# A drain of GpSimd's pipe behind each of its additions, in a planned attention-and-mixer kernel

## The chip, the cores and the metric

One core of a Trainium2 chip runs the kernel. It has five engines, each with an instruction queue of its own: TensorE (PE; its weight loads are listed as PEld), VectorE (DVE), ScalarE (ACT), GpSimd (POOL) and SyncE (SP), which issues most DMAs. The metric is the device time of one execution in microseconds (us); lower is better. Three runs of the kernel before gave a median of 793.61 us (793.22 to 793.68).

## The reference

A routed attention is followed by an MLP mixer. Batch 4, 8 heads, sequence 768, head dimension 64, 16 clusters; then model width 512, token width 256, channel width 1536. All in float32.

```python
q_assign = np.argmax(np.einsum('bhsd,hcd->bhsc', q_n, c_n), axis=-1)
k_assign = np.argmax(np.einsum('bhsd,hcd->bhsc', k_n, c_n), axis=-1)
mask = q_assign[:, :, :, None] == k_assign[:, :, None, :]
scores = scale * np.matmul(q, k.transpose(0, 1, 3, 2))
scores = np.where(mask, scores, -1000000000.0)
...
attn = attn / (np.sum(attn, axis=-1, keepdims=True) + 1e-09)
out = np.matmul(attn, v)
...
xt = x.transpose(0, 2, 1)
h = np.maximum(xt @ w_tok1, 0.0) @ w_tok2
u = x + h.transpose(0, 2, 1)
h2 = np.maximum(u @ w_ch1, 0.0) @ w_ch2
return u + h2
```

`x` is the attention's output with the heads side by side, 4 x 768 x 512.

## The kernel before

The kernel works out a whole program first and then plays it out. Each operation is added to a `Program` with the engines that may take it, a cost for each, and the buffers that it reads and writes. `plan()` then goes through them as a list scheduler does: TensorE's operations keep the order in which they were added; for the other engines it takes, at each moment, the ready operation with the earliest due time, and gives it to an engine that would finish it first. `Program.run` issues the result, so every engine's order is fixed before anything runs. Costs are a constant and a part per element, from the table `COST`; `cost(e, n)` reads it. The scheduler holds GpSimd's and VectorE's operations on arena operands apart, since it counts the two as sharing a port.

All data stand in one buffer of the on-chip memory, the arena, and in eight PSUM banks (`ps`). Stages in order of time: attention in 16 pairs of heads (to some 350 us), token mixing (`token1`, `token2`, to some 405 us), then for each of two groups of two batches `channel1` and `channel2`, the two channel matrices. Every one of these four products is done by a Strassen-like scheme of seven `product` calls. Each `product` is itself such a scheme of seven smaller ones: its four sums T1 to T4 of the right-hand operand are made by `tsum`, its weights come from DRAM through a ring of eight buffers, and for each of its seven parts three matmuls of 128x384 go into PSUM, which VectorE (or ScalarE) then evacuates, mostly by adding what is there already. The sums use two sets of buffers in turn.

GpSimd takes part only here. In `channel1` it makes all `tsum` sums and the `combine` sums between the products (T3, T4, `a` plus `c`, `c` plus `b`, and some of T1 and T2); in `channel2` it makes the `tsum` sums of the first two products, and VectorE the others. Each of its additions covers 128x384 float32, in the arena, and all go through the helper `tt` at L881, whose instruction is at L883: 179 of them. Behind its last sums of a group, `channel2` has VectorE overwrite the matrices that those sums read (`combine(Hm[0, 0], ...)`, on VectorE), and VectorE's queue holds the evacuations of PSUM that TensorE waits for.

ScalarE does the relus between the two matrices (L890) and, in the same time, a check that the weights are in range (L1888); both are placed by the scheduler too.

Of the kernel before, what the change touches and what calls it, by code (L numbers as in the profile page):

```python
# [55 lines left out]
    "ACT16": (-0.275, 0.001426),  # L56
    "JOIN16": (-0.165, 0.001426),
    "DVE": (0.075, 0.00104),
    "POOL": (0.12, 0.0023),
}  # L60
ISSUE = 0.63
BUS = 240e3
# [660 lines left out]
def kernel(  # L723
# [26 lines left out]
    nc = tc.nc  # L750
# [105 lines left out]
    def cost(kind, n):  # L856
        a, b = COST[kind]
        return a + b * n
# [22 lines left out]
    def tt(dst, a, b, op, n, rd, wr, engines=("DVE",)):  # L881
        def fn(e):
            (nc.vector if e == "DVE" else nc.gpsimd).tensor_tensor(out=dst, in0=a, in1=b, op=op)  # L883

        return g.add({e: cost(e, n) for e in engines}, fn, rd, wr)

# [184 lines left out]
    def route(m, bk):  # L1071
# [13 lines left out]
        def blocks(t):  # L1085
# [3 lines left out]
        vec(lambda: nc.vector.reduce_max(out=mxs.ap[:, 0:24], in_=blocks(a), axis=AX.X), 0.54,  # L1089
            a.k(), mxs.k())  # L1090
        tt(blocks(e), blocks(a), mxs.ap[:, 0:24].unsqueeze(2).to_broadcast([P, 24, C]),
           ALU.is_ge, HS, a.k() + mxs.k(), e.k())
        vec(lambda: nc.vector.transpose(out=o.ap, in_=e.ap), 0.56, e.k(), o.k())
# [107 lines left out]
    def add_up(m):  # L1201
        st = unit[m]
        for n in range(2):
            a = es[n]
            x, y, z = st[HJ * n : HJ * n + HJ]
            tt(a.ap, x.ap, y.ap, ALU.add, 2 * S, x.k() + y.k(), a.k())
            tt(a.ap, a.ap, z.ap, ALU.add, 2 * S, a.k() + z.k(), a.k())
        a, b = es[1], es[0]
        if FOLD[m] == "V":
            tt(a.ap, a.ap, b.ap, ALU.add, 2 * S, a.k() + b.k(), a.k())  # L1210
        if FOLD[m] != "T":
            return

        def fn(e):
            nc.gpsimd.dma_start(
                a.ap.rearrange("p h t -> p (h t)"), b.ap.rearrange("p h t -> p (h t)"),
                accum_op=ALU.add,
            )

        g.add({"POOL": 1.0}, fn, a.k() + b.k(), a.k(), (2.2 * 768 * 1024, 6144))  # L1220
# [812 lines left out]
```

## Time and profile before

| what | value |
|---|---|
| median of three runs | 793.61 us |
| the profiled execution's own time | 794.77 us |
| its span, first to last instruction | 793.0 us |
| TensorE clock granted, mean | 0.999 |
| TensorE's idle time from 370 to 400 and from 400 to 450 us | 0.51 and 0.39 us |
| GpSimd's first and last addition begin at | 374.03 and 699.48 us |
| last instruction of TensorE ends at | 787.4 us |

In the profile, L883 is a line of the kernel; "out<-in" are the names of buffers. An idle time belongs to the instruction behind it and is put down to what ended it ("<-"). The chain of waits goes back from the last instruction, at each step to what released it.

### The profile page before, as it was taken

The page shows a single profiled execution, that of the slowest core. Times are in us where ns is not written, and L with a number is a line of the kernel's source. Part 1 is how long each engine was busy: PE and PEld are TensorE (multiplying, and loading weights), DVE is VectorE, ACT ScalarE, POOL GpSimd, SP SyncE. Part 2 cuts the span into 40 slices and gives each one's busy share as a digit, 9 for nine tenths or more (in the row PEclk, how much of TensorE's full clock was granted, in tenths as well). Part 3 has the DMA queues.
Part 4 walks back from the last instruction along what each step waited for, and adds up shares of the span by engine and source line. Part 5 has one row for each costly group of instructions (what it writes and reads, how often), then busy time and mean ns, then how long its engine had stood idle before and what let it go on. Part 6 is the DMA issues. An engine that isn't in the chain of part 4 may idle for free.

```text
span 793.0 us, 15364 instructions
## 1 busy us (share of the span) xinstructions
PE 780.1 (98%) x5983; PEld 465.4 (59%) x5983; DVE 677.5 (85%) x876; ACT 461.2 (58%) x612; POOL 190.2 (24%) x185
## 2 busy tenths in 40 slices
PE   7999999999999999999999999999999999999997
PEld 6666666666666666544555555555555555555554
DVE  6869999999999999999999967899953567799964
ACT  4688898888898875599714367642245204400422
POOL 0000000000000000001264599700186379830000
PEclk9999999999999999999999999999999999999999
DMA  9576769777678953659858999975788844444767
GB/s 214 154 174 164 183 151 232 205 219 203 162 207 183 273 180 113 182 110 224 184 139 246 312 290 258 270 191 123 167 188 179 170 106 102 100 101 106 162 144 178
DMA packets 326576, 143.68 MB, mean 181 GB/s; under 512 B 260192, under 2 KB 322400, under 8 KB 326496
## 3 DMA queue, kind: packets, MB, share of 16 engines
q1 hardware_dynamic: 324128, 141.83, 71.4%
q8 instruction: 49, 0.80, 0.4%
q10 hardware_dynamic: 2368, 0.79, 0.4%
q14 instruction: 31, 0.25, 0.1%
HBM read 91.95 MB, written 28.61 MB: 152 GB/s over the span
## 4 chain that ended last, share of the span: by engine, by line
PE 88%; DVE 5%; ACT 3%; issue 2%; DMA 1%; SPq 0%; POOL 0%; DVEq 0%; POOLq 0%; ACTq 0%
PE ps L844 72%; PE ps L1226 16%; DVE arena L883 4%; ACT arena L873 2%; DMA wd<-arena 1%; ACT arena L1193 1%; DVE arena L865 0%; DVE arena L1360 0%; SPq L903 0%; DVE arena L1363 0%; ACT arena L863 0%; DVE arena L1366 0%; DVE arena L1356 0%; DVE arena L1280 0%; DVE arena L1273 0%
## 5 line engine op out<-in xcount | busy, mean ns | idle before, releaser
L844 PE MATMUL ps<-arena 128*128 128x384 f32 (+5 forms) x2735 | 642.4, 463 | 7.3 <-DVE arena L865 2.7
L844 PEld LDWEIGHTS ps<-arena 128*128 128x128 f32 (+1 forms) x2351 | 342.3, 185 | 252.8 <-issue 59.5
L883 DVE TENSOR_TENSOR arena<-arena 128x1536 f32<-128x1536 f32 (+6 forms) x350 | 370.2, 1079 | 10.5 <-PE ps L1226 2.3
L883 POOL TENSOR_TENSOR arena<-arena 128x384 f32<-128x384 f32 x179 | 189.5, 1094 | 510.8 <-DVE arena L883 379.4
L883 DVE TENSOR_TENSOR arena<-ps,arena 128x384 f32<-128x384 f32 (+3 forms) x227 | 189.6, 845 | 79.4 <-PE ps L844 75.4
L873 ACT COPY arena<-arena 128x768 uint16<-128x768 uint16 x221 | 189.4, 953 | 61.4 <-DMA arena<-arena 31.9
L1193 ACT ACTIVATE arena<-ps 128x768 f32<-128x768 f32 x192 | 150.6, 811 | 31.6 <-PE ps L844 29.9
L1226 PE MATMUL ps<-arena 128*32 128x192 f32 (+1 forms) x3248 | 144.7, 335 | 0.0
L1226 PEld LDWEIGHTS ps<-arena 128*32 128x32 f32 x3248 | 103.8, 110 | 44.0 <-issue 13.9
L863 ACT COPY arena<-ps 128x384 f32<-128x384 f32 (+2 forms) x41 | 29.5, 728 | 120.6 <-PE ps L844 120.4
L890 ACT ACTIVATE arena<-arena 128x1152 f32<-128x1152 f32 (+1 forms) x38 | 39.9, 1075 | 54.9 <-DVE arena L883 54.5
L1888 ACT ACTIVATE arena<-arena 128x768 f32<-128x768 f32 x40 | 38.7, 970 | 32.7 <-DMA arena<-in_moe_w_ch_dram 24.7
L844 PEld LDWEIGHTS <-arena 64*128 64x128 bf16 x384 | 19.3, 94 | 25.0 <-issue 0.6
L1360 DVE SCALAR_TENSOR_TENSOR arena<-arena 128x512 uint32<-128x512 uint32 (+1 forms) x31 | 20.6, 681 | 0.3
L1097 ACT ACTIVATE arena<-arena 128x384 bf16<-128x384 f32 x16 | 11.2, 703 | 16.1 <-issue 16.1
L1366 DVE SCALAR_TENSOR_TENSOR arena<-arena 128x512 f32<-128x512 uint32 (+1 forms) x31 | 20.2, 671 | 0.4
L1356 DVE TENSOR_SCALAR arena<-arena 128x512 uint32<-128x512 uint32 (+1 forms) x31 | 13.2, 435 | 5.8 <-DMA arena<-in_moe_w_tok_dram 5.8
L1273 DVE STREAM_TRANSPOSE arena<-ps 128x768 f32<-128x768 f32 x16 | 15.3, 955 | 0.0
L1363 DVE TENSOR_SCALAR arena<-arena 128x512 uint32<-128x512 uint32 (+1 forms) x31 | 14.4, 483 | 0.3
L865 DVE COPY arena<-ps 128x384 f32<-128x384 f32 (+3 forms) x12 | 8.0, 666 | 4.7 <-PE ps L844 4.6
L1088 DVE STREAM_TRANSPOSE arena<-ps 128x384 f32<-128x384 f32 x16 | 9.2, 575 | 3.1 <-PE ps L844 3.0
L1280 DVE STREAM_TRANSPOSE arena<-ps 128x384 f32<-128x384 f32 x16 | 9.3, 579 | 1.5 <-PE ps L1226 1.2
(58 smaller groups left out, 53.1 us busy)
## 6 DMA issues: line engine op xcount, KB each, us to landing
arena<-wd SPq DMA_DIRECT2D x196, 192.0 KB, 3.0
wd<-arena SPq DMA_DIRECT2D x84, 224.0 KB, 3.2
arena<-in_moe_w_ch_dram SPq DMA_DIRECT2D x96, 128.0 KB, 3.0
arena<-in_moe_w_ch_dram SPq DMA_DIRECT2D x16, 768.0 KB, 6.0
arena<-in_v_dram SPq DMA_DIRECT2D x16, 384.0 KB, 4.7
out_dram<-arena SPq DMA_DIRECT2D x14, 384.0 KB, 3.6
arena<-in_k_dram SPq DMA_DIRECT2D x13, 384.0 KB, 4.0
arena<-in_q_dram SPq DMA_DIRECT2D x13, 384.0 KB, 4.2
```

The costliest lines, as they stand in the source:

```text
L844: nc.tensor.matmul(dst, lhsT=lhsT, rhs=rhs, start=start, stop=stop, tile_position=pos, is_transpose=tr, skip_group_check=True,)
L863: nc.scalar.copy(out=dst, in_=src)
L873: nc.scalar.copy(out=dst, in_=src)
L883: (nc.vector if e == "DVE" else nc.gpsimd).tensor_tensor(out=dst, in0=a, in1=b, op=op)
L890: nc.scalar.activation(out=dst, in_=src, func=ACT.Relu)
L1193: lambda e, ex=ex, s=s, u=u: nc.scalar.activation(out=ex.ap[:, :, u * HS : (u + 1) * HS], in_=ps[:, 2 * s : 2 * s + 2, 0:HS], func=ACT.Exp ...
L1226: nc.tensor.matmul(dst, lhsT=lhsT, rhs=rhs, start=start, stop=stop, tile_position=pos, skip_group_check=True,)
L1273: lambda: nc.vector.transpose(out=x.ap[:, :, cols].rearrange("p j (c d) -> p c j d", d=32), in_=ps[:, 6:8, 0:HS],),
L1360: vec(lambda: nc.vector.scalar_tensor_tensor(out=TT, in0=hi, scalar=0xC0000000, in1=hh, op0=ALU.bitwise_and, op1=ALU.bitwise_or), 0.14 + 0 ...
L1363: vec(lambda: nc.vector.tensor_scalar(out=hh, in0=TT, scalar1=0xFF800000, scalar2=None, op0=ALU.bitwise_and), f, T.k(), h.k())
L1366: vec(lambda: nc.vector.scalar_tensor_tensor(out=ll, in0=lo, scalar=float(2.0**-52), in1=hh.bitcast(F32), op0=ALU.mult, op1=ALU.mult,), 0. ...
L1888: lambda e, i=i, func=func, bias=bias, n=n, hi=hi: nc.scalar.activation(out=hi, in_=hi, func=func, bias=bias, accum_out=wsum.ap[:, i, n : ...
```

## The change

GpSimd's branch of `tt` issues a drain behind its addition, and the planner's constant for a GpSimd operation goes from 0.12 to 0.2. A drain is an instruction that holds GpSimd's queue until the engine has finished what was issued before it. The drains carry no semaphore, waits or updates; the instructions that depend on an addition still wait for the addition itself.

```diff
@@ COST @@
-    "POOL": (0.12, 0.0023),
+    "POOL": (0.2, 0.0023),
@@ tt @@
         def fn(e):
             (nc.vector if e == "DVE" else nc.gpsimd).tensor_tensor(out=dst, in0=a, in1=b, op=op)
+            if e == "POOL":
+                nc.gpsimd.drain()
 
         return g.add({e: cost(e, n) for e in engines}, fn, rd, wr)
```

Since the planner reads the new constant, the built program differs in more than the drains. TensorE's order is the same. GpSimd has 179 additions in both, 107 of them ahead of its one other late instruction, a load of a flag, before and 105 after. VectorE's order differs from the last part of token mixing on, ScalarE's from the first range checks on, and SyncE's loads of weights and of the range check are interleaved anew.

## The prediction

> **What bounds the kernel now.** I read the page's totals first, then the chain of waits, then stretches of time, then GpSimd's timeline.
>
> ```profile
> span 793.0 us, 15364 instructions
> PE 780.1 (98%) x5983; PEld 465.4 (59%) x5983; DVE 677.5 (85%) x876; ACT 461.2 (58%) x612; POOL 190.2 (24%) x185
> L883 POOL TENSOR_TENSOR arena<-arena 128x384 f32<-128x384 f32 x179 | 189.5, 1094 | 510.8 <-DVE arena L883 379.4
> ...
> 415.33 370.91 PE ps L844 x1154
> 786.24 0.02 issue
> ```
>
> TensorE sets the time. From 415.33 on the chain is one unbroken piece of 1154 matmul records, up to 786.24. GpSimd (POOL) is busy 24% of the span and all its 179 large instructions come from L883, the line the change edits. So the question is whether slower additions on GpSimd can open a hole in those 370.91 us. The next table asks where GpSimd is full.
>
> ```profile
> 370.00:400.00 30.00, 29.49 (x90) 16.38 (x89) 28.87 (x59) 20.91 (x25) 9.00 (x9) 1.00 0.83 193
> 400.00:450.00 50.00, 49.61 (x153) 28.45 (x152) 47.87 (x61) 18.53 (x27) 24.76 (x24) 1.00 0.76 220
> ...
> 449.97:480.13 30.16, 30.16 (x95) 17.81 (x94) 21.38 (x17) 17.24 (x27) 30.15 (x31) 1.00 1.06 281
> 480.13:512.00 31.87, 31.87 (x100) 18.73 (x99) 24.77 (x22) 23.16 (x36) 28.08 (x25) 1.00 0.96 268
> 512.00:571.00 59.00, 59.00 (x185) 34.75 (x184) 57.82 (x66) 19.35 (x33) 0.00 (x0) 1.00 0.71 173
> 571.00:606.00 35.00, 35.00 (x111) 20.44 (x110) 16.34 (x24) 16.93 (x19) 29.06 (x27) 1.00 0.78 178
> 606.00:639.95 33.95, 33.95 (x107) 19.92 (x106) 19.98 (x15) 10.39 (x11) 9.65 (x11) 1.00 0.75 159
> 639.95:702.00 62.05, 62.05 (x194) 36.57 (x193) 46.21 (x37) 18.07 (x16) 58.78 (x56) 1.00 0.45 103
> 702.00:760.00 58.00, 58.00 (x182) 34.03 (x181) 55.63 (x57) 10.40 (x15) 0.00 (x0) 1.00 0.56 129
> ```
>
> Columns after the stretch and its length: busy time of PE, PEld, DVE, ACT, POOL. Two stretches are full on GpSimd: 449.97 to 512 (31+25 = 56 additions, 58.23 us busy of 62.03) and 639.95 to 702 (56 additions, 58.78 of 62.05). They are the second half of the first channel product of each group and the start of the second one. Right behind each, VectorE (DVE) is full: 57.82 of 59.00, and 55.63 of 58.00. TensorE has no idle time in either, so there is nothing to win there, only to lose. In 370 to 450 TensorE idles 0.51 + 0.39 = 0.90 us: all that a luckier order could win before the tail.
>
> **The change, part by part.** *What stays.* TensorE's order is the same instruction for instruction, GpSimd still gets 179 additions, no semaphore is added, and each drain waits for nothing but the pipe. Up to about 400 us every engine's order is the same, so nothing earlier can move.
>
> *The drains.* 179 drains, one behind each addition. What an addition costs now, and what it costs where it can't overlap its predecessor:
>
> ```profile
> 375.99 1.01 POOL L883 TENSOR_TENSOR arena<-arena 128x384 f32<-128x384 f32 x1
> ...
> 377.08 1.00 POOL L883 TENSOR_TENSOR arena<-arena 128x384 f32<-128x384 f32 x1
> ...
> 639.95 38.33 POOL L883 TENSOR_TENSOR arena<-arena 128x384 f32<-128x384 f32 x40 [2.27 <-DVE arena L883]
> 679.19 1.00 POOL L883 TENSOR_TENSOR arena<-arena 128x384 f32<-128x384 f32 x1 [0.91 <-PE ps L844]
> 681.13 8.77 POOL L883 TENSOR_TENSOR arena<-arena 128x384 f32<-128x384 f32 x9 [0.93 <-PE ps L844]
> 690.87 10.73 POOL L883 TENSOR_TENSOR arena<-arena 128x384 f32<-128x384 f32 x6 [0.97 <-PE ps L844]
> ```
>
> 40 in a row take 38.33 us: 0.96 us from start to start, although one takes 1.00 us, so neighbours overlap by 0.04 us. The addition at 377.08 needs the result of the one at 375.99 (the fourth sum T4 reads the second, T2), which ends at 377.00: it starts 0.08 us later, a pitch of 1.09. A drain is at least such a wait. Its own cost shows only at the program's ends:
>
> ```profile
> 0.34 0.10 POOL L2017 MEMSET const-uint8-127<- 128x1 uint8 x1
> ...
> L2017 POOLq DRAIN  x1: 186/186/186, 0.3 to 0.3; - x1
> ...
> L2028 POOLq DRAIN  x3: 34/45/82, 701.7 to 792.7; - x3
> ...
> L883 POOLq EVENT_SEMAPHORE  x11: 17/17/43, 451.9 to 500.8; - x11
> ```
>
> The drain that found work in the pipe ran from 0.30 to 0.49, 0.05 us past the last memset's end (0.34 + 0.10). So behind an addition: 1.00, plus 0.05 until the drain ends, plus the 0.08 of a released start: 1.13. GpSimd also handles 11 separate semaphore waits among the 56 additions of a full stretch; now they run under the addition before, behind a drain they stand bare, each with its 17 ns and another start of 0.08: 11 x 0.10 / 56 = 0.02. I take a pitch of 1.15. Bounds: below 1.03 (1.00 and the shortest drain, 34 ns, the rest overlapped); above 1.21 (1.00, the whole 186 ns as added, and the 0.02). 1.15 sits between, next to the dependent pair's 1.09 and the one drain that had to wait.
>
> The Trainium skill (page "VectorE: DVE Perf Modes", section "The DRAIN you can't avoid") says of the drains at a program's ends that they take a constant 12 ns or so on all five engines. By that figure a drain would add an estimated 0.01 us to the pair's 1.09, and nothing would be lost below; GpSimd's own rows, 34 to 186 ns, are dearer than that here.
>
> *The planner's number.* The kernel orders its own work; it charged an addition 0.12 + 384 x 0.0023 = 1.003 us and now charges 1.083. So it puts VectorE's and ScalarE's dependents 0.08 us per addition later, and other work before them: from about 400 us on, VectorE's sums, evacuations and weight rounding, ScalarE's relus and range checks and SyncE's (SP's) loads are interleaved anew. The moved weight loads have eight ring buffers and the DMA engines' share was 0.45 to 1.06; I cost the moved loads at nothing while the ring covers them. The reordering itself I cost at 0, with bounds of plus and minus the 0.90 us above. What it does cover is GpSimd's lateness up to a pitch of 1.083; beyond, 1.15 - 1.083 = 0.067 us per addition builds up unplanned, 56 x 0.067 = 3.75 us by the end of each full stretch.
>
> *Who is late next.* Behind an addition GpSimd holds the next sums for TensorE; those are handed over some products ahead through two sets of buffers. The tight hand-over is at the end of each full stretch, where VectorE overwrites the matrix that GpSimd's last sums read:
>
> ```profile
> 687.94 1.00 POOL L883 TENSOR_TENSOR arena<-arena 128x384 f32<-128x384 f32 x1
> ...
> 690.10 1.35 DVE L883 TENSOR_TENSOR arena<-arena 128x1152 f32<-128x1152 f32 x1
> ...
> DVE arena L883 <- POOL arena L883: 2.4, 4, 0.6
> L844 PE MATMUL ps<-arena 128*128 128x384 f32 x1146 | 370.5, 486 | 0.4 <-DVE arena L883 0.4
> 694.63 0.56 DVE L883 TENSOR_TENSOR arena<-ps,arena 128x384 f32<-128x384 f32 x1
> ```
>
> VectorE's combination at 690.10 needs the read that ends at 688.94: 1.16 us of slack. VectorE works in order, so queued behind it are the evacuations of the PSUM banks, and TensorE waits for those. One group of six records takes 6 x 370.5 / 1146 = 1.94 us and its evacuation 0.56, so an evacuation may be late by at most 1.38, less two hand-overs; I take 1.2. Lateness that reaches TensorE: 3.75 - 1.16 - 1.2 = 1.4 us per full stretch; VectorE's idle time behind (1.18 and 2.37 us) comes after the hole is made. Other GpSimd work (24.76 of 50.00, 29.06 of 35.00, 9.65 of 33.95) waits for TensorE anyway and costs nothing.
>
> *Sum.* 2 x 1.4 = 2.8 us. The profiled execution took 794.77 us, 1.8 more than its span, and 1.2 more than the median of the runs; on it the sum is 797.6. On the median, 793.61 + 2.8 = **796.4 us**.
>
> **The rivals.** (1) *Not slower:* the new plan covers it. The hole opens only when 56 x (pitch - 1.083) exceeds 1.16 + 1.2, that is from a pitch of 1.125 on. If the drain overlaps a little with the next instruction's wait, the pair's 1.09 is the answer and the time is 793.6. For it: the pair, the new charge, the short drains of 34 to 82 ns. Against: the drain that had to wait outlasted the memset by 0.05 by itself. (2) *Faster:* the new order closes the 0.90 us of holes before 450: 792.7, and so still inside the 0.2% (1.6 us), about what a measurement of this kernel can tell from no change. Against more than that: TensorE is full behind it. Only the tail of 793.0 - 786.24 = 6.8 us is left, with its last stores in a slightly different order. (3) *Dearer, through the operands' port:* of the six additions from 690.87, four took about twice the time (10.73 for six) while VectorE combined arena operands. If GpSimd's lateness pushes four more of its additions under VectorE's combinations in each full stretch, each costs 1.1 more, 4.4 per stretch, with the slack already spent: 2.8 + 8.8, 805 us. For it: GpSimd will run 56 x (1.15 - 0.96) = 10.6 us more per stretch against some 3.5 us of idle time. Against: the plan moves those combinations later as well.
>
> The Trainium skill (page "SBUF — State Buffer", section "SBUF: two separate sides") states that GpSimd and a VectorE instruction with two SBUF inputs lock a shared pair of ports for a whole instruction. The 10.73 us agree with it.
>
> **How the numbers follow.** Main case 0.52; not slower, 0.28; faster or a won order 0.06, of it 0.04 beyond 0.2%; dearer 0.14. The range: below, 793.61 - 0.9 = 792.7; above, a pitch of 1.21 gives 56 x 0.127 = 7.1, less 2.36 is 4.75 per stretch, 9.5 in all: 803.1. The main case's own range is 795.2 to 800. Slower by over 0.2%: nearly all of the main and dearer cases, 0.65; within: 0.31; faster: 0.04.
>
> **What would show it.** Right: additions in a row 1.13 to 1.17 us apart; new TensorE idle time of 1 to 2 us near 500 to 530 and near 690 to 730, released by VectorE evacuations that stand behind a combination waiting for GpSimd; the rest of the chain unbroken. Wrong: a pitch under 1.12 with no hole (rival 1), or over 1.25; additions of 2.1 us much more often than now (rival 3); holes at other places, at 400 to 450 above all, or a wait for a weight load, which would mean that the reordering, not the drain, decides.

## The result, and the profile after

The changed kernel took 800.84 us (median of four runs, 800.45 to 801.42); the kernel before, beside it, 793.64 us. The ratio is 1.0092 with a 95% interval of 1.0074 to 1.0109: slower by 7.2 us, where 2.8 had been forecast. The profiled execution took 801.42 us, 1.8 more than its span; it is the longest of the four.

The page of the changed kernel: its span, busy times, GpSimd's group, and the chain of waits by engine. The last row is the drains' own, from the view of their line (count, shortest/median/longest in ns).

```profile
span 799.6 us, 15534 instructions
PE 782.4 (98%) x5983; PEld 464.6 (58%) x5983; DVE 682.6 (85%) x878; ACT 458.8 (57%) x610; POOL 199.7 (25%) x185
PE 68%; POOLq 15%; DVE 10%; issue 4%; ACT 1%; DMA 1%; ACTq 0%; SPq 0%; DVEq 0%
L883 POOL TENSOR_TENSOR arena<-arena 128x384 f32<-128x384 f32 x179 | 199.0, 1112 | 514.9 <-DVE arena L883 385.1
L885 POOLq DRAIN  x179: 1069/1096/2304, 372.5 to 713.2; - x179
```

The chain that was one piece of TensorE from 415 us on now runs through GpSimd's queue (POOLq, the drains) for 15% of the span and through VectorE for 10%. A drain's row of 1.1 us isn't its price: the row lasts about as long as the addition (1.00 us) that the drain waits for. The price stands between the additions, as the pitch, the time from one start to the next. GpSimd's timeline:

```profile
686.25 1.00 POOL L883 TENSOR_TENSOR arena<-arena 128x384 f32<-128x384 f32 x1 [0.16 <-POOL arena L883]
687.41 1.00 POOL L883 TENSOR_TENSOR arena<-arena 128x384 f32<-128x384 f32 x1 [0.16 <-issue]
...
694.36 1.01 POOL L883 TENSOR_TENSOR arena<-arena 128x384 f32<-128x384 f32 x1 [0.16 <-issue]
695.59 1.00 POOL L883 TENSOR_TENSOR arena<-arena 128x384 f32<-128x384 f32 x1 [0.22 <-POOL arena L883]
```

From 686.25 to 687.41 are 1.16 us from start to start, where it was 0.96 before. The 0.04 us of overlap has become 0.16 us of nothing, and 0.22 where a separate semaphore wait stands in front.

The same full and idle stretches as before, by windows (PE, PEld, DVE, ACT, POOL; granted clock, DMA share, GB/s):

```profile
449.97:512.00 62.03, 62.03 (x194) 36.50 (x193) 43.45 (x35) 41.20 (x65) 53.27 (x51) 1.00 0.98 268
512.00:523.00 11.00, 8.95 (x24) 4.87 (x23) 8.07 (x8) 5.84 (x13) 8.64 (x6) 0.85 0.98 290
523.00:571.00 48.00, 48.00 (x150) 28.28 (x149) 46.75 (x54) 11.90 (x18) 0.00 (x0) 1.00 0.62 140
...
644.00:715.00 71.00, 71.00 (x221) 41.79 (x220) 50.62 (x42) 19.28 (x19) 61.60 (x56) 1.00 0.45 103
715.00:760.00 45.00, 43.10 (x133) 24.87 (x132) 44.61 (x45) 9.50 (x13) 0.17 (x1) 1.00 0.54 123
```

Each of GpSimd's full stretches is longer than its 62 us of before: of the first one's 56 additions, 51 begin by 512, and the second one's take 71.00 us. TensorE is unbroken within the second, and loses time right behind each: 2.05 us of 11.00 at a granted clock of 0.85, and 1.90 of 45.00. TensorE's own timeline has the places:

```profile
499.70 17.90 PE L844 MATMUL ps<-arena 128*128 128x384 f32 x55
519.65 40.68 PE L844 MATMUL ps<-arena 128*128 128x384 f32 x120 [2.05 <-POOL arena L883]
...
719.45 9.94 PE L844 MATMUL ps<-arena 128*128 128x384 f32 x30 [1.37 <-DVE arena L883]
729.92 3.49 PE L844 MATMUL ps<-arena 128*128 128x384 f32 x10 [0.52 <-DVE arena L883]
```

A record takes 486 ns and the next one starts after 323 (370.5 / 1146), so a hole (a stretch in which TensorE stands idle) costs its idle time and 0.16 us: 2.2 at 519.65, 1.5 and 0.7 at 719.45 and 729.92. The 120 records from 519.65 on should take 119 x 0.323 + 0.486 = 38.9 us and take 40.68. The missing 1.7 us are in the first 3.35 of them, at half the clock:

```profile
519.65:523.00 3.35, 3.35 (x6) 1.83 (x7) 3.35 (x4) 2.08 (x4) 1.78 (x1) 0.50 0.87 258
```

Together 2.2 + 1.7 + 1.5 + 0.7 = 6.1 of the 6.6 us between the spans. The places were forecast; the size of the first and the half clock were not.

The half clock belongs to this execution, though, and not to the change as such. The mean granted clock of the four executions was 0.996 (the profiled one), 1.000, 0.999 and 0.998. Half a clock for 3.35 us takes 0.002 off the mean, so the two at 1.000 and 0.999 can't have had it, and they still took 801.01 and 800.45 us.

### The profile page after: what moved, and what is told of

It is laid out like the page before. It is cut to its first block, busy times and chain, and to the rows that moved or that the text cites. A ratio compares the mean times of both kernels' runs of the same rounds, so it can differ in the third digit from the quotient of the medians.

```text
span 799.6 us, 15534 instructions
## 1 busy us (share of the span) xinstructions
PE 782.4 (98%) x5983; PEld 464.6 (58%) x5983; DVE 682.6 (85%) x878; ACT 458.8 (57%) x610; POOL 199.7 (25%) x185
## 4 chain that ended last, share of the span: by engine, by line
PE 68%; POOLq 15%; DVE 10%; issue 4%; ACT 1%; DMA 1%; ACTq 0%; SPq 0%; DVEq 0%
PE ps L844 52%; PE ps L1228 15%; POOLq L885 15%; DVE arena L883 8%; ACT arena L873 1%; DMA arena<-in_moe_w_ch_dram 0%; DMA arena<-wd 0%; DVE arena L1368 0%; DVE arena L865 0%; DVE arena L1275 0%; DVE arena L1282 0%; DVE arena L1362 0%; ACTq L905 0%; ACT L984 0%; DVE arena L1365 0%
## 5 line engine op out<-in xcount | busy, mean ns | idle before, releaser
L883 DVE TENSOR_TENSOR arena<-arena 128x1536 f32<-128x1536 f32 (+6 forms) x350 | 374.8, 1092 | 14.5 <-POOL arena L883 5.2
L883 POOL TENSOR_TENSOR arena<-arena 128x384 f32<-128x384 f32 x179 | 199.0, 1112 | 514.9 <-DVE arena L883 385.1
L863 ACT COPY arena<-ps 128x384 f32<-128x384 f32 (+2 forms) x40 | 28.3, 718 | 125.6 <-PE ps L844 125.4
L1099 ACT ACTIVATE arena<-arena 128x384 bf16<-128x384 f32 x16 | 11.2, 703 | 15.5 <-issue 15.5
L1358 DVE TENSOR_SCALAR arena<-arena 128x512 uint32<-128x512 uint32 (+1 forms) x31 | 12.3, 408 | 6.0 <-DMA arena<-in_moe_w_tok_dram 6.0
L1365 DVE TENSOR_SCALAR arena<-arena 128x512 uint32<-128x512 uint32 (+1 forms) x31 | 13.0, 439 | 0.3
```

Of the source, the lines that this page charges most:

```text
L863: nc.scalar.copy(out=dst, in_=src)
```

## The experiments

The theory was the prediction's: GpSimd's pitch, beyond what the plan covers, makes it late at the end of each full stretch, VectorE waits for it there, and PSUM evacuations behind that wait come late for TensorE. The rivals were the reordering by the planner's new number, a price of the drain that no plan can hide, and, once the hole at 519.65 was seen, ScalarE. Medians, and ratios to the kernel before run beside them (793.8 to 794.2 us):

| kernel | us | ratio, 95% interval |
|---|---|---|
| drains, constant 0.12 | 810.78 | 1.0214 [1.0200, 1.0228] |
| drains, constant 0.2 (the change) | 800.84 | 1.0092 [1.0074, 1.0109] |
| drains, constant 0.29 | 796.40 | 1.0026 [1.0016, 1.0037] |
| constant 0.2 alone | 794.77 | 1.0009 [1.0000, 1.0019] |
| constant 0.2, a no-operation in place of the drain | 794.68 | 1.0007 [0.9998, 1.0016] |
| a drain behind every other addition | 795.55 | 1.0020 [1.0011, 1.0028] |
| two drains behind each | 809.50 | 1.0199 [1.0186, 1.0212] |
| drains outside the full stretches | 795.59 | 1.0016 [1.0005, 1.0027] |
| drains in the first full stretch only | 797.73 | 1.0059 [1.0046, 1.0071] |
| the change without the later range-check loads | 800.73 | 1.0087 [1.0073, 1.0101] |
| constant 0.2 alone, without these loads | 795.17 | 1.0016 [1.0007, 1.0025] |

**The two halves of the change.** First the drains with the planner's old number, then the new number without drains.

```diff
-    "POOL": (0.2, 0.0023),
+    "POOL": (0.12, 0.0023),
```

> The drains of the change, with the planner's old constant 0.12 for GpSimd, so the order of before. Theory (the drain keeps neighbouring additions from overlapping, 1.16 us from start to start against 0.96, and what the plan did not charge reaches TensorE): the plan charges 1.003 us, so 56 x 0.16 = 9 us per full stretch are unplanned, less some 2.4 us of slack, 6.6 us twice, and holes of TensorE of several us at 505 to 520 and at 700 to 720: 806 to 811 us, slower than the change. Rival (the new order is what costs): with the old order back the time falls to 794 to 796 us.

```diff
             (nc.vector if e == "DVE" else nc.gpsimd).tensor_tensor(out=dst, in0=a, in1=b, op=op)
-            if e == "POOL":
-                nc.gpsimd.drain()
```

> The planner's constant 0.2 alone, without drains, so the change's order at the old pitch of 0.96 us. Theory (drains cost, order does not): 792.7 to 794.5 us, and no hole of TensorE behind 450 us. Rival (the order costs): 798 to 801 us, with holes near 520 and 720.

810.78 and 794.77 us. Without the plan's cover the drains cost 16.6 us. TensorE's timeline of that kernel:

```profile
509.84 10.46 PE L844 MATMUL ps<-arena 128*128 128x384 f32 x27 [6.14 <-POOL arena L883]
...
707.28 12.97 PE L844 MATMUL ps<-arena 128*128 128x384 f32 x34 [5.71 <-POOL arena L883]
```

Two holes, at the two places forecast, of 6.3 and 5.9 us with the 0.16; the rest is half clock again (27 records should take 8.9 us and take 10.46; 34 should take 11.2 and take 12.97). The new number by itself costs 0.7 us by the ratio, with an interval that begins at none; the result lies 0.3 above the theory's range and 3 below the rival's. So the reordering isn't the cause, and the two halves don't add up: the new number alone wins nothing and takes 10 us off the drains' cost.

**More cover.** Drains, with 0.29 in the plan: 1.173 us per addition, just above the measured pitch.

```diff
-    "POOL": (0.2, 0.0023),
+    "POOL": (0.29, 0.0023),
```

> The drains with the planner's constant at 0.29, that is 1.173 us per addition, about what the changed kernel's additions took from start to start. Theory (the loss is lateness that the plan does not know of): GpSimd is as slow as in the change, 1.16 us, but what waits for it is planned behind it; 793 to 796 us. Rival (GpSimd has become a bound that no order hides: 56 x 1.17 = 65.5 us of additions in a stretch that was 62 us): 799 us or more, with the same holes.

796.40 us. TensorE from 450 us to its end:

```profile
449.74 337.95 PE L844 MATMUL ps<-arena 128*128 128x384 f32 x1052
788.02 0.55 PE L844 MATMUL ps<-arena 128*128 128x128 f32 x3 [0.33 <-DVE arena L883]
```

Every drain is still there, at the same pitch, and no hole is left behind 450. What remains (2.2 us by the medians, 1.1 by the spans) lies ahead of it, where this order opens idle times of 0.42, 1.05 and 0.56 us between 402 and 430. It misses the theory's upper end by 0.4 and the rival's lower end by 2.6. So the drain's time as such doesn't make the loss; lateness that the plan doesn't know does.

**Is it the waiting, or one more instruction?** In place of the drain, an instruction of the engine that does nothing.

```diff
-                nc.gpsimd.drain()
+                nc.gpsimd.engine_nop()
```

> The change's order, and behind each addition an empty instruction that goes to the engine and waits for nothing, in place of the drain. Theory (it is the wait for an empty pipe that costs): additions in a row stay at or under 1.02 us from start to start, 793 to 795 us. Rival (one more instruction in the queue costs, of whatever kind): 1.10 us or more from start to start, 797 us or more.

794.68 us, the time of the new number alone. GpSimd's timeline:

```profile
640.42 25.53 POOL L883 TENSOR_TENSOR arena<-arena 128x384 f32<-128x384 f32 x26 [2.26 <-DVE arena L883]
```

(25.53 - 1.00) / 25 = 0.98 us from start to start: 0.02 for the instruction. So the other 0.18 of a drain isn't the price of one more instruction in the queue. The second drain below costs 0.04 to 0.07 with nothing left to wait for; the wait makes the rest.

**Dose and place.** A drain behind every other addition; two behind each; only outside the two full stretches (additions 1 to 31 and 88 to 123); only in the first (32 to 87).

```diff
             if e == "POOL":
+                nadd[0] += 1
-                nc.gpsimd.drain()
+                if nadd[0] % 2:
+                    nc.gpsimd.drain()
```

> The change's order, a drain behind every other addition alone. Theory (only what goes beyond the charge of 1.083 us reaches TensorE): the mean from start to start is (0.96 + 1.16) / 2 = 1.06 us, under the charge, so the loss is gone nearly whole: 793.5 to 795.5 us, no hole of TensorE behind 450 us over 0.5. Rival (each drain costs its share of the 7.2 us): half of them cost 3.6 us, 797 to 798.5 us.

```diff
                 nc.gpsimd.drain()
+                nc.gpsimd.drain()
```

> The change's order, two drains behind each addition. The second finds the pipe empty and shows what of the 0.20 us is the instruction and what the refilling of the pipe. Theory (drain and following start are worked through one after the other): 0.05 to 0.09 us more, 1.21 to 1.25 us from start to start, 56 x 0.07 = 4 us more lateness in each full stretch, 807 to 811 us. Rival (a drain of an empty pipe is hidden): 1.16 us as in the change, 800 to 802 us.

```diff
-                nc.gpsimd.drain()
+                if nadd[0] <= 31 or 88 <= nadd[0] <= 123:
+                    nc.gpsimd.drain()
```

> The change's order, drains behind the 67 additions outside the two full stretches alone (the 1st to 31st and the 88th to 123rd of 179). Theory (GpSimd waits for TensorE there anyway, the drains lie in its idle time): 793.5 to 795.5 us, holes as with the charge alone. Rival (the loss comes from the crowded start of the channel products, 400 to 450 and 571 to 606 us): 797 us or more.

```diff
-                nc.gpsimd.drain()
+                if 32 <= nadd[0] <= 87:
+                    nc.gpsimd.drain()
```

> The change's order, drains behind the 56 additions of the first full stretch alone (the 32nd to 87th). Theory (each full stretch makes its own holes): the hole of 2 us near 520 us and the slow records behind it come back, those near 720 and 730 us don't; 3 to 5 us over the charge alone, 797.5 to 799.5 us. Rival (lateness is carried on from one group to the next): the whole loss or nearly none of it, 800 to 801.5 us or 794 to 795.5 us.

795.55, 809.50, 795.59 and 797.73 us. Half the drains cost under 1 us over the new number alone, the whole 6, twice as many 15: a threshold, not a price per drain. The first time lies 0.05 above the theory's range and 1.45 below the rival's. The second drain adds 0.04 to 0.07 to the pitch, and the hole behind the first stretch is followed by half clock here too (36 records should take 11.8 us):

```profile
649.96 1.00 POOL L883 TENSOR_TENSOR arena<-arena 128x384 f32<-128x384 f32 x1 [0.21 <-issue]
651.16 1.00 POOL L883 TENSOR_TENSOR arena<-arena 128x384 f32<-128x384 f32 x1 [0.21 <-issue]
652.39 1.00 POOL L883 TENSOR_TENSOR arena<-arena 128x384 f32<-128x384 f32 x1 [0.23 <-issue]
```

```profile
510.03 13.54 PE L844 MATMUL ps<-arena 128*128 128x384 f32 x36 [1.94 <-issue]
```

The 67 drains outside the full stretches add no hole to those of the new number alone; they land 0.1 above the theory's range, and their interval against before overlaps that of the new number alone. The 56 of the first stretch make holes only behind it, of 0.62, 0.85, 0.48 and 0.32 us between 517 and 538 and none at the second, 3.0 us above the new number alone. That is in the theory's range, but the hole of 2 us and the half clock that it forecast didn't come. VectorE is as late there as in the change (the combination that waits for GpSimd begins at 514.86, in the change at 514.93), so the difference lies elsewhere; the next experiment has it. What drains in the second stretch alone would cost was not measured; the change's trace shows 2.2 us there.

**ScalarE at the first hole.** The profile puts the hole at 519.65 down to GpSimd, but the matmul there needs a PSUM bank that ScalarE evacuated. ScalarE's timeline in the changed kernel, and then in the one with the new number alone, which has the same order:

```profile
517.08 0.92 ACT L1890 ACTIVATE arena<-arena 128x768 f32<-128x768 f32 x1 [3.73 <-DMA arena<-in_moe_w_ch_dram]
...
519.10 0.46 ACT L863 COPY arena<-ps 128x384 f32<-128x384 f32 x1
```

```profile
513.10 0.93 ACT L1888 ACTIVATE arena<-arena 128x768 f32<-128x768 f32 x1 [2.63 <-DMA arena<-in_moe_w_ch_dram]
...
515.73 0.48 ACT L863 COPY arena<-ps 128x384 f32<-128x384 f32 x1 [0.48 <-PE ps L844]
```

The copy of L863 waits for TensorE in the one (515.73), and stands at 519.10 behind a range check that waits for its load in the other; 519.10 + 0.46 = 519.56, and TensorE goes on at 519.65. ScalarE's relus now wait 19.2 us for GpSimd (1.4 with the new number alone), which makes the range checks late, and the next load into one of their two buffers:

```profile
ACT arena L892 <- POOL arena L883: 19.2, 8, 7.9
```

That is only half of it. The load for the check at 517.08 was issued at 508.92; with the new number alone its counterpart was issued 1.8 us earlier, at 507.16. From issue to check went 8.2 us in the change and 5.9 there. With drains in the first stretch only, the load was issued at 509.04, as late as in the change, yet its check began at 515.37, after 6.3 us. So the hole needed a slow load besides, whose cause stays open.

So two kernels left out the range-check loads from the third block on, with the change and with the new number alone.

```diff
-                dma(
-                    araw.ap.rearrange("p n two -> p (n two)"),
-                    flat[:, 2 * WP * c : 2 * WP * (c + 1)], [], araw.k(), 768, 6144, 418.0,
-                )
+                g.add(
+                    {"SP": ISSUE},
+                    lambda e, n=n, c=c, araw=araw, flat=flat: nc.sync.dma_start(
+                        araw.ap.rearrange("p n two -> p (n two)"),
+                        flat[:, 2 * WP * c : 2 * WP * (c + 1)],
+                    ) if n < 2 else None,
+                    [], araw.k(), (768 * 1024, 6144), 418.0,
+                )
```

> The change (drains, constant 0.2) with only the first two range-check loads issued: all later pairs of range-check activations run on what already stands in the two buffers, so ScalarE keeps all of its activations in their order and none of the later ones can wait for a load. The weights from the third block on are not checked. Theory (the hole at 519.65 is made by ScalarE: GpSimd's late sums hold its relus, those hold the range checks in front, the next load into the same buffer is issued late, and the PSUM copy behind the waiting range check comes late): that hole and the half clock behind it go, 2.2 + 1.7 = 3.9 us, while the holes near 720 and 730 (2.2 us) stay; about 797, between 796 and 798. Rival (the hand-over from GpSimd to VectorE, which waits 3.2 us at 514.9, makes the hole, and the loads have no part in it): the hole near 519 stays over 1.5 us and the time stays at 800 to 801.5.

> The kernel with the constant 0.2 alone, without drains, and with only the first two range-check loads issued; the weights from the third block on are not checked. It is what the run without loads has to be set against. Theory: nothing waits for these loads without the drains, so the time stays where the constant alone puts it, 794.0 to 795.2. Rival (the loads cost time by themselves, by their share of the DMA engines or of the queue): faster than 793.5, and then that much has to be taken off what the run with drains wins.

800.73 and 795.17 us: the first forecast failed by 3 us. The time is the rival's, but the rival's hole at 519 isn't there. ScalarE's copy, TensorE and VectorE in the change without these loads:

```profile
516.34 0.48 ACT L863 COPY arena<-ps 128x384 f32<-128x384 f32 x1 [2.88 <-PE ps L844]
```

```profile
499.69 20.48 PE L844 MATMUL ps<-arena 128*128 128x384 f32 x63
521.38 4.14 PE L844 MATMUL ps<-arena 128*128 128x384 f32 x12 [1.21 <-DVE arena L865]
526.00 11.88 PE L844 MATMUL ps<-arena 128*128 128x384 f32 x36 [0.48 <-DVE arena L883]
538.20 2.20 PE L844 MATMUL ps<-arena 128*128 128x384 f32 x6 [0.32 <-DVE arena L883]
```

```profile
515.23 1.36 DVE L883 TENSOR_TENSOR arena<-arena 128x1152 f32<-128x1152 f32 x1 [2.04 <-POOL arena L883]
...
520.78 0.54 DVE L865 COPY arena<-ps 128x384 f32<-128x384 f32 x1
```

The copy is on time, and the hole at that matmul and the half clock behind it are gone. In their place stand three holes that VectorE ends, 1.21 + 0.48 + 0.32 + 3 x 0.16 = 2.5 us, which in the changed kernel lay hidden behind the first. By the traces that wins 3.9 - 2.5 = 1.4 us in this stretch; against that, TensorE's work ahead of 403 us ended 0.6 us later in this trace, for a cause that stays open. By the medians it wins nothing (800.73 and 800.84), which fits: at least two of the change's four executions had no half clock to lose. Set against the new number alone without loads, the change costs 5.6 us by the medians, against 6.1 with them; the intervals are too wide to tell the two apart. ScalarE's wait is what ended the first hole in the profiled execution, but VectorE's was close behind it. That GpSimd's lateness made the load's issue late is read from the trace, not tried by itself.

No kernel tried is faster than the one before.

## Why the prediction was right, and where its size was off

**The time:** 800.84 us lies in the stated range, 792.7 to 803.1, but 0.8 above the main case's own, 795.2 to 800. The upper end came from a pitch of 1.21, which wasn't reached. With the measured pitch the prediction's own sum is 2 x (56 x 0.077 - 2.36) = 3.9 us, so 797.5. The other 3.3 us come from steps that it had otherwise, told below, and that they fit under the upper end is luck.

**Where GpSimd is full, and what can only be lost there:** right. Drains elsewhere add no hole.

**The pitch:** 1.15 forecast, 1.16 measured, inside the bounds of 1.03 and 1.21. The row that gave it, the one drain that had to wait, was the right one. The dependent pair's 1.09 was too low, and with it the first rival (no loss below 1.125) fell. The figure of the Trainium skill (page "VectorE: DVE Perf Modes", section "The DRAIN you can't avoid"), 12 ns, is for the drains at a program's ends; a drain behind work on GpSimd cost 0.20 us here.

**The separate semaphore waits:** forecast at 0.10 each behind a drain; 0.06 measured (0.22 against 0.16).

**The reordering:** 0 forecast within 0.9 either way; 0.7 measured for the new number alone, its interval from 0 to 1.5. The second rival, a luckier order, didn't come.

**The lateness at the hand-over:** forecast 3.75 - 1.16 = 2.59 us. It can be measured against the kernel with the new number alone, since that has the same order. VectorE there, and then in the changed kernel, at the second hand-over:

```profile
700.45 0.56 DVE L883 TENSOR_TENSOR arena<-ps,arena 128x384 f32<-128x384 f32 x1 [0.99 <-PE ps L844]
700.92 3.32 DVE L883 TENSOR_TENSOR arena<-arena 128x1152 f32<-128x1152 f32 x2
704.16 1.01 DVE L883 TENSOR_TENSOR arena<-ps,arena 128x384 f32<-128x384 f32 x2
705.10 2.61 DVE L883 TENSOR_TENSOR arena<-arena 128x1152 f32<-128x1152 f32 x2
708.18 3.90 DVE L883 TENSOR_TENSOR arena<-arena 128x1152 f32<-128x1152 f32 x3 [0.48 <-PE ps L844]
712.12 0.56 DVE L883 TENSOR_TENSOR arena<-ps,arena 128x384 f32<-128x384 f32 x1
```

```profile
704.57 0.56 DVE L883 TENSOR_TENSOR arena<-ps,arena 128x384 f32<-128x384 f32 x1 [0.69 <-PE ps L844]
...
708.69 1.36 DVE L883 TENSOR_TENSOR arena<-arena 128x1152 f32<-128x1152 f32 x1 [2.04 <-POOL arena L883]
709.96 1.02 DVE L883 TENSOR_TENSOR arena<-ps,arena 128x384 f32<-128x384 f32 x2
710.90 8.03 DVE L883 TENSOR_TENSOR arena<-arena 128x1152 f32<-128x1152 f32 x5
718.85 0.54 DVE L883 TENSOR_TENSOR arena<-ps,arena 128x384 f32<-128x384 f32 x1
```

The evacuation that TensorE releases is 704.57 - 700.45 = 4.12 later: that is TensorE's loss so far. The two behind the hand-over are 709.96 - 704.16 = 5.80 later, so VectorE is 1.7 us late, by its wait for GpSimd. The next evacuation, at 718.85, is 6.73 later, 2.6 late: in between stand five combinations, the first of them beside GpSimd's last additions. At the first hand-over the same two evacuations, and TensorE, with the new number alone, and then the evacuations in the changed kernel:

```profile
513.64 1.01 DVE L883 TENSOR_TENSOR arena<-ps,arena 128x384 f32<-128x384 f32 x2
...
499.73 72.13 PE L844 MATMUL ps<-arena 128*128 128x384 f32 x223
```

```profile
516.21 1.01 DVE L883 TENSOR_TENSOR arena<-ps,arena 128x384 f32<-128x384 f32 x2
```

They are 2.6 apart, with TensorE level (its stretches begin at 499.73 and 499.70, with no hole in either until 517). So 2.6 and 1.7 at the hand-overs: that term held at the first and was 0.9 too large at the second. What it was made of is another matter; see the port below.

**The slack of an evacuation** (how late it may be before TensorE waits): here is the step that failed: "an evacuation may be late by at most 1.38, less two hand-overs; I take 1.2", taken off once per stretch. For the first hole it holds: 2.6 late and a hole of 1.5 at 719.45 make a slack of 1.1, and the 1.4 that the prediction had per stretch is about this hole. But VectorE is full behind the hand-over (46.75 of 48.00 us, 44.61 of 45.00), keeps its lateness, and reaches evacuations with less slack, at 729.92 in the second stretch and 526.00 and 538.20 in the first without the loads. So nearly all of VectorE's lateness reaches TensorE: 2.2 and 2.5 us, not 1.4 each. With no slack taken off, the prediction's own sum is 2 x 2.59 = 5.2 us; the reordering's 0.7 comes on top.

**What the prediction hadn't named:** ScalarE's queue at 519.65 and the half clock behind that hole. In the profiled execution they make the first stretch 3.9 us where VectorE alone made 2.5; the median doesn't rest on the half clock. "A wait for a weight load" stood in the prediction as a sign that the reordering decides; a load for the range check did end a wait, but with the same order and no drains it ended none on TensorE's path.

**The port (third rival):** it came in part, and its share stays open. GpSimd's additions took 18 ns more in the mean (1112 against 1094), 3.2 us over the 179, where the rival wanted 8.8. But the mean hides the place. Thirteen additions took 1.9 us or more, against seven before and six with the new number alone; eleven of the thirteen stand in the full stretches, where the new number alone has four. GpSimd at the second hand-over, with the new number alone and then in the changed kernel:

```profile
690.88 10.88 POOL L883 TENSOR_TENSOR arena<-arena 128x384 f32<-128x384 f32 x9 [0.99 <-PE ps L844]
```

```profile
700.28 1.91 POOL L883 TENSOR_TENSOR arena<-arena 128x384 f32<-128x384 f32 x1 [0.16 <-POOL arena L883]
...
705.59 1.91 POOL L883 TENSOR_TENSOR arena<-arena 128x384 f32<-128x384 f32 x1 [0.16 <-issue]
707.66 1.00 POOL L883 TENSOR_TENSOR arena<-arena 128x384 f32<-128x384 f32 x1 [0.16 <-issue]
708.82 2.09 POOL L883 TENSOR_TENSOR arena<-arena 128x384 f32<-128x384 f32 x1 [0.16 <-POOL arena L883]
```

VectorE waits for the addition at 707.66. The six additions up to it, from 699.13 on, took 9.5 us, where the pitch makes 5 x 1.16 + 1.00 = 6.8; at the first hand-over six took 10.0. With the new number alone the same six took 6.9 both times, where 0.96 makes 5.8. So some 1.6 and 2.1 us of GpSimd's lateness come from additions that were slow beside VectorE's combinations, about as much as the 1.7 and 2.6 that reached VectorE. Behind the second hand-over VectorE pays too: its five combinations took 8.03 us, and 2.61 + 3.90 = 6.51 with the new number alone. So the drains start the lateness, but how much of the loss is pitch and how much is the port, no run here tells apart; that 3.75 - 1.16 came out near 2.6 is in part luck.

## What to carry to other kernels

A fixed cost per instruction on a side engine costs nothing until that engine is late at a hand-over; so look for the stretch in which it is full, and tell the planner the measured pitch, not the price on paper. When lateness is passed to an in-order engine that is itself full, the slack of the first wait is no gain: it comes out at the next tight one, until that engine has idle time. A wait that the trace names may hide another of nearly the same size: what its removal wins is known only from a run. And a profile is one execution: compare its clock with that of the others before a loss that it shows is put down to the change.

## What the runs showed of the hardware

**Half clock behind short holes.** Expected time of a group of records as above (323 ns each, 486 for the last) against the one shown, for the groups behind a hole:

| hole, idle us | kernel | records | expected, shown us | lost us |
|---|---|---|---|---|
| 6.14 and 5.71 | drains, 0.12 | 27; 34 | 8.9, 10.46; 11.2, 12.97 | 1.6; 1.8 |
| 2.05 | the change | 120 | 38.9, 40.68 | 1.7 |
| 4.38 | two drains | 40 | 13.1, 14.77 | 1.7 |
| 1.94 | two drains | 36 | 11.8, 13.54 | 1.7 |
| 1.37 | the change | 30 | 9.9, 9.94 | 0.1 |
| 1.21 | without loads | 12 | 4.0, 4.14 | 0.1 |

Behind these idle times of 1.94 us and more TensorE ran at half its clock for some 3.2 to 3.6 us (twice what was lost; the windows at 519.65 show 0.50), behind 1.37 and less it did not; a hole of 2 us so cost nearly twice its length. The Trainium skill (page "TensorE: Matmul & The Clock Gate", section "What's actually happening") states that half rate comes after at least one idle window of about 3.4 us. Here 1.94 us were enough.

**The price of a drain on GpSimd.** 0.20 us from start to start behind an addition of 1.00 us, 0.06 more with a separate semaphore wait in front, 0.04 to 0.07 for a second drain, and 0.02 for an instruction of the engine that does nothing.
